# A new order table for a fused attention and feed-forward kernel on one core, and its last stores shared anew

## The chip, the core and the metric

The kernel runs on one core of one Trainium2 chip. A core has TensorE (matmuls, the page's PE, with its weight loads shown apart as PEld), VectorE (DVE), ScalarE (ACT), GpSimd (POOL) and SyncE (SP), and sixteen DMA engines. The metric is the device time of one execution in microseconds. Each run counts once; the median of the runs is compared.

## The reference, cut to what matters

```python
B, N, m, C = 4, 12480, 32, 128            # tokens: 4 x 12480 = 49920
def mab(q, kv):                           # attention
    s = (1 / sqrt(C)) * (q @ kv.T)
    a = exp(s - s.max(-1)); a /= a.sum(-1) + 1e-9
    return a @ kv
h = mab(inducing, x)                      # 32 x 128 for each of the 4 batches
y = mab(x, h)                             # 12480 x 128 for each batch
u = y @ w_in                              # 128 -> 2048
g = maximum(u, 0) + alpha * minimum(u, 0)
out = g @ w_out                           # 2048 -> 128, float32
```

## The kernel before, in words

Since `y = a @ h` with only 32 rows in `h`, the kernel folds `h @ w_in` into one 32 x 2048 matrix for each batch (`hW`, made in `h_weights`). A token's hidden values are then a matmul with 32 rows of contraction from its 32 unnormalized attention weights (`rep`), and a quarter of TensorE's array holds it. The leaky activation is split into a linear part, one matmul with `hA` straight from the attention weights (`linear`), and a ReLU part. The division by the sum of the weights comes last, on the output.

The tokens are cut into 100 groups, 25 to a batch: 24 of 512 tokens and one of 192. Each group has sixteen chunks of 128 hidden values (for the small group, two chunks share one eviction, so that it has eight). For every chunk a **fill** (`fill`, L733) makes one matmul into a bank of PSUM, and one engine evicts the bank with a ReLU into a bf16 tile `gt`: ScalarE at L750, VectorE at L752. Then the **second matmul** (`second`, L784) multiplies `gt` by `W1` and accumulates the 128 outputs in a bank that the group holds until it ends.

TensorE's array is split in four tiles of 32 rows, named w, x, y, z. A second matmul is cut into four, one on each tile, 32 hidden values each; they all add into the same bank. So tile w does all its sixteen of a group first, then x its sixteen, and so on, and between two tiles stands a **hand-over** (`hand_over`, L723): a no-operation in TensorE's queue that waits until the tile before has ended its last matmul of that group. The last three groups (`WHOLE`) aren't cut: their second matmuls take the full array.

When a group's last second matmul is out, `finish` (L809) transposes the bank on VectorE into `ot`, multiplies it by the reciprocal sums on GpSimd into `ob`, and stores `ob` with four DMAs of 32 partitions, on GpSimd's queue. For the last groups (`to_end` counts how many groups have yet to end) the scaling is shared with VectorE and the four stores go out on other queues. `ob` has three buffers, `ot` two.

The order of all this is written out by hand, or rather by characters, in the table `PLAN`. Every engine's instructions are pinned to the order in which the table names them:

- `a` to `h` with a digit: a fill on tile w (a, b), x (c, d), y (e, f) or z (g, h) into the bank of that number; the first letter of each pair evicts on ScalarE, the second on VectorE.
- `w`, `x`, `y`, `z`: the next second matmul of that tile. Each tile walks through the groups by itself.
- `v`: the next second matmul on the full array, in the last three groups. `l` and `m` with a digit: a group takes that bank, and its linear matmul on tile w opens it (`l` for the cut groups, `m` for the last three).
- `s` with digits: a **stop**, at which the table `PAUSES` has attention scores, denominators and the like done on the full array. [...]

A **letter** below is one entry of the table, its bank digit included. A group has 64 second matmuls, sixteen fills and one linear matmul, 81 letters.

Of the kernel before, what the change touches and what calls it, by code (L numbers as in the profile page):

```python
# [200 lines left out]
b02h12c223a312s4h212b012a323c12313f413s23e01h112l2wg42d33w231w3e03w32d1w31we431w3f31w3e01w32w3d1  # L201
2w3c42w32wd3g02w132w12h1wc4232xa02h3xa523x23b4x23a1x23xl0w23wxxwf3g5xw3e4s1h5xe3wxe4w3xwf13xw23x
wxe3wh5x2w32wc43wyd13wyc6wg3ys5b4yya1d6ywya5yyg3xb43xy3ya1xyxh6yc53yxh3ya4x3xy3xb1xza6zl5xe7zwxf
3zwc4wzwf1zxwe6zwh7xwzc3wzxwg4d1wzxwe6xzwf7zwzc3ywywzd4ywzc1yzl6yxwg7yxg3wxywh4xywxya1xywxyh2a7x
ywxyb3xya4xywd1ywxe2wxzf7s342zf1xwzxwe3zxwf7zwc2zwyc4zwyd1zwyzyc3zyxb7zyxg2yxb4zyxza1yxzyxb3ze7x
zyxl2yxwg4yxwyxwg1yxwh3yxwxg7wf4xzwxe0zwze1wzywd3zywzyc7wzyd4wzyc0wzwf1zwyza3yza7xyzb4xyza0xzyxl
1zyxwyxwg3yxwh7xywg4yxwh0xywg5xwzxe3wxzwf7xzwxze4wxf5zwc0zwzd3yws745d0wzywyzc3b7yzyzxa4yzxl5yzxb
0yzxa3yzxwzxywxg7ywxg4ywyxh0wyg3xwyxwyxh7wxe6wxzf4wxze0wxze3wzwd7zywc6zywzywd4zyc0zyxb3zyxzya7xz
yb6xzya4xzyl0xzywxg3ywxzywxg7ywxyh6wxywg4xe3wxzwxf2zwxzwe7xzwe4d6zwyzwyd3zwyzc2wyzd7wyza6yzl4xyz
wxyg3b2xyzxwyza6xyzb7xyzwxyg3wxyg2wxyh6ywxwxwxe7zs312xzb7e6xzwf3xzwe2xzwzwc1zywd6yzwc7yzwd2yzwza  # L210
3yzyb1xyzxa6zyxl7zyxwh2yxa3yxzwyxwg6yxwg1yxwyxwh3yxwg2xwe6xwzf5xwzxwze1xwzf3c2wzwzywd6yzwc5yzyzd
1yzb3xyzxa2yzxa6yxzl5yxzwyxza1yxzwyxg2wyxh3wyxg6wyxwyxh1wxe0wxze2wxzwxf3zwze6wzywzyc0wzyd1wzywc2
zyd3l6zyxwzya0xzyb1xzywxzya2zxyzxwys3012xh4ywxg3ywxywh0xywg2xe1wxwzf4xwzxwe3zxwzf2xwzc0wzd1wyzwy
c4zyza3yzxb2yzxl0yzxwyzc1b4yzxwyzxa3yzxwyg2xwyxwh1yxg4wyxwyxg3wyd7wxwe2zxwf1zxwzxwe4zxwf3zc7wzc2
ywzyd1zyxzya4xzb3yxza7yxzyxb2zyxzl1yxg4wyxwh3yxwg7yxzwyxzwyc2ywxg4yxwf3xwze7xwzxwf2s5437wyzd2wyz
c5wyzwyzd4we3zwyzb7yza2yzxya5zxyb4zxyl3zxywxzf7a2xzywxzywxg5ywxg4ywxyh2wxg7wxwxzf5wxze6wxze4wxzw
zd2wzywzc7ywzd6ywzyc5za4yzb2xyzxyl7zxywzxyb6g5xywzxywzxya4xywg2xywh6xywxywg5xwf4xwze0xwzf2xwze6x
wzwzd5ywzc4ywzc0ywzyl6zd2wzyxwzyxzya4xzyb5xzya0xzywxg2ywxzywxywh4xywg5xywxyg0wxs2154wxe0zwxf2zwx
e1zxwze4d5zwzywd0zywc2zyl1yzxwyzxa5zyxb4zyxwyzc2b0yzxwyzxa5yxwzyxwg4yxwg2yxwh0yxwyxwg5xwf4xzwe3x
zwxzwf2c0zwzd5ywyzwyzc4l3yzwxzya2xzyb0xzywxe5zwd4yzwxzya2xzywxzya0xywxh5ywxg4ywxywxg2ywxh0wxe7zw  # L220
xf4zwxzwe5c2zwyzwd0yzl7ywzxya4xzf5wzxywyzc2b0yzxwyzxa4yzxb5yzxwzyc2wzyxs0452ywxg0f6wxg4ywxg5ywxh
2ywxs0d6we4zxwzxwze5xwzf2c0wzd4zyl6yxzwxyza5xyzb2xyzwc0yzwxyzb4xyza5xyzwxyza2xyzwxywg0xyh4wxyg5x
wys21045wxywxh2e1wxf4zwc5zwyzwyc0zwyd1zwyc2zyzb5xyza4xyzl0xyzwxyza1xf2zwxzywxf4g5wxyzwxyza1xzywx
yg2wxyg5wxyh4wxwxf1zwxe3zwzwc2yzwyd5wzyc4wzyzl3d1yzwxyza2xyzwxf5zwxe4zwxyzb1xyza2xywzxyzwc5ywxyg
4wxyg1b2xywxywxe5b7xzwe4xzwd2zwxe1zwd5zwyc7zwyzc4yb2zxyl1zxywzxya5h7yxwzyxwg4d2ywzywxza5yxzyb7xz
xywg4ywxzywxg2yxwe5wxf7wzxf4xzws2657wxzf2wzc4wzyd6wzyc7l5zywwzxywwwzxe2b4zxywwzxywa7h6xywwxzywwx
zwe2wb4xyzwxwzya7xzyl6xywxg2ywxyh4wxywg7xywxwf0c2zwyxzxwxyxh4wc7yzxwyxzxwxe2d0zwyxzxwyxzwc7f4zxw
yxzxwyc2zb0yxzxxyza7xyzb4xyzxya2zxyzl0xywg7xywxyh4ywyxe2zwxyzwyxyyh3we7xzwyxyzywyxe4h2wxyzwyxyyz
wyc7f3zwyzwyc4zwyd2zwyzwc7yzyb3zxya4zxyzxa2yzxl7yzxzwyzzxa3zf4zxzwzyzxzwzyg2xywh1xwyzxg3wyxzzwxz
ze4wzxf2wzxwe1zxwzf3c5wzywzyc4wzyd2wzyc1zwyb3zyza5xyzxyb4zxya2zxyl1xzywxze3xwyh5xwyg4xwyxwyg2xwy  # L230
h3s6452xzwf3xzwe6xzwe4xzwf2xzwc5zwzwyd3wzywd6zywc4zya2zyl5zyxwh3yxwzyxwg4yxb6zyxwzyxa2yzxwyxwyg3
xwyxh4ya6xwe2xwxzf0wxzwxe3zwxzf6wzc4wzywd2zywc0zyzya3zxb6yzxyl4zxywzc2b0yzxywzxya3zxywg6xywxyh2w
xywg0xyg3wxywh7xwe6xzwxzwf2xzwe0xzwd3zwyzc7wyzwyza6d2yzl0xyzwxyg3wd7yzwxyzwxe6zb2xyzwxyza3xyzwxy
a7xywh6xyg2wxywxyg3wxf1wxwzxe7wzxf2zwc6zwyzwd3yzc1yzxa7yzxb2yzxl6yzxwyzc3b1yzxwyzxwyg7xb2yzxwyzx
we3zwxyg1wxywxywxh7ys23517xwzf2xwze3xwzf7c5wzwzyc1wzyd2wzya3zyzyxb7zyxa5zyxb1zyxl2zyxwze3xwzyd7w
yxg5wyxzwyxg1wyxg3wyxh7wyxwxg5wxzf1wxze4wxzwzd3wzyc7wzyd5wzyc1l4zyxwzyxa3zf7xwzyxwze1xzb5yxzwyxz
a3yxzwyxg7wyxwh1yxa5yxwg3yxwyxh0wyxwe7xwzf5wc1zywzywd3zywc0zya7zyxb5zyxl1zyxwzyc3b0zyxwzyxwg7f5x
wzyxwzyxa3zf0xwzyxwg7yxwzyxwg5yxwf3xwe0zxwzxwze7wd6zywzywc5yzd0l3zwxe7zwxzyb6xzywc5yzwxyzxb0yzxa
7zyxwyh6xa5yzxwyzxwyg0xwyxwg7yxwyh5xws60275h6we0xwzxwzd2e5zyc7wzywzyd0l6zyxwzyxa5zyd2wzyxwg7yxwz
f0xwzyxa5zyxwh2yxwze7xwzyxwh0yxa5yzxwyxza2yxg7wxwzxf0wze5wzywd2zywc4zya7zyxzb0yxzl5yxzwyxg2b4yxz  # L240
wyxzwyc7h0wyxzwyxza2yxh4wyxzwyc7zwyxzwe0xwf2zxwzxe4wzxwzxe7wzd0wzywzc1yl4zd2ywzxya7zxywh0xywzc1y
wzyxb2zyxa7zyxwzyxa0zyxwg1yxwyxwh2yxwg7yxwxf0we3xzwf1xzwze2xwzwzc7wyzd0yl3zwyxzya2xh1ywxzxya7zxy
b0zxywzc2wyzd1wyzxa7yzwxyzwxyg0wxyh2xwyg1wxye7wxwxzf0s6127f0zxwe6zxwzd1we7zwyzc2yzxyb0zxyzxya6zy
xb7zyxa1zyxl2zyd0wzyxwg6yxwh7yxwzyc1wzyxwg0yxwh6xywxwe7xzwxe1zwxzwf0c5zwyzwd7yzwc6yzwd1yza0yzxl5
yzxwyzxa7f6zxwyzxwyg0xb1yzxwyzxa7yzxwyg6xwyh0xwyxg1wyxwe7xwzxf4wzxe6wzwzyd1wzyc0wzyd7wzya4zya6xz
yxzb1yxzl0yxzwyd7zwe4xzwyxzwe6xzwyxg1wyxwh4yxwyg7xwyxh6wyxa3xe1wzxwzf4xwze7wzywzd3ywzc6yl1zyxwh4
yxwg7yxwzyxb3zyc6wzyxwzyxa4h7yxwzyxwzyd3a6zyxwzyxwg4yxwzxe7wzxwzxb6s34273e6wzd4f7wzxe2wzxs3yc6wz
yl4zd2ywzxya7zxzb3yxg6wyxywzxwyh2xyg7wxzwyxzb3yc6ywzxyzwxza2yxyg7wxwyxf6xg3wxwze2xwzf5zwzwyc7zwy
# [59 lines left out]
def kernel(  # L308
# [815 lines left out]
```

## Time and profile before

| | us |
|---|---|
| median of 3 runs | 541.08 |
| lowest and highest run | 541.07, 543.59 |
| span of the profiled execution | 540.4 |
| TensorE matmuls busy | 526.3 |
| VectorE, ScalarE, GpSimd busy | 504.2, 496.3, 394.7 |

The profiled execution's own time is its span, from its first to its last instruction; the page gives no other. The median of the runs lies 0.7 us above it. TensorE's granted clock is full throughout (0.996 on the mean). Matmuls overlap on the four tiles and their ends are modelled, so TensorE's busy share does not say how full it is; starts do. A row such as `bank<-gt,W 32*128 32x512` is a second matmul on one tile, `bank<-rep,hW` a fill, `bank<-rep,hA` a linear matmul, and `128*128` a matmul on the full array. In the timeline, neighbouring instructions of one name are merged into one row with their count.

### The profile page before, as it was taken

The numbers are of one execution on the slowest core, as the hardware profiler recorded it, in microseconds if no ns is written. First come the engines' busy times: TensorE is split into PE (matmuls) and PEld (weight loads), VectorE is DVE, ScalarE is ACT, GpSimd is POOL, SyncE is SP. The second block draws the span as 40 slices with busy tenths as digits, with TensorE's granted clock in tenths as the row PEclk, the third lists the DMA queues.
The fourth block names the chain that finished last, engine by engine and source line by source line (L and its number), as shares of the span: only waits on it lengthen the run. The fifth ranks groups of instructions, "written<-read, shape, count | busy, mean of one in ns | idle before, by whom it ended". The sixth has DMA issues, their size and how long they took to land.

```text
span 540.4 us, 21603 instructions
## 1 busy us (share of the span) xinstructions
PE 526.3 (97%) x8988; PEld 332.7 (62%) x8988; DVE 504.2 (93%) x865; ACT 496.3 (92%) x994; POOL 394.7 (73%) x574
## 2 busy tenths in 40 slices
PE   4999999999999999999999999999999999999996
PEld 4655566566567566666667666666666566666653
DVE  3699999999989999999998999999999999999994
ACT  2499999999989999999999999999999999999950
POOL 5553778687667987687687987776767876776764
PEclk9999999999999999999999999999999999999998
DMA  8999999987799898887799797864354344334324
GB/s 197 212 186 139 182 185 156 170 142 113 112 175 149 134 160 152 162 129 145 117 153 166 117 164 158 168 101 113 66 93 113 66 96 112 70 89 108 68 42 85
DMA packets 114738, 71.12 MB, mean 132 GB/s; under 512 B 86784, under 2 KB 102784, under 8 KB 114640
## 3 DMA queue, kind: packets, MB, share of 16 engines
q0 software_dynamic: 19456, 38.62, 38.9%
q1 hardware_dynamic: 91984, 30.22, 32.9%
q8 instruction: 70, 1.15, 0.9%
q10 hardware_dynamic: 3200, 0.90, 0.7%
q14 instruction: 28, 0.23, 0.2%
HBM read 41.00 MB, written 28.95 MB: 129 GB/s over the span
## 4 chain that ended last, share of the span: by engine, by line
PE 90%; DMA 4%; DVE 2%; ACT 1%; POOL 1%; issue 1%; SPq 0%; POOLq 0%; DVEq 0%
PE bank L383 90%; DMA xn<-in_x_dram 2%; DMA rep<-e2d 1%; ACT gt L750 1%; DVE gt L752 1%; DMA e2d<-e 1%; POOL xn L412 0%; DVE ot L818 0%; PE bank L458 0%; ACT e L656 0%; DVE xT L461 0%; POOL ob L826 0%; DVE fr L608 0%; SPq L671 0%; POOL out_dram L851 0%
## 5 line engine op out<-in xcount | busy, mean ns | idle before, releaser
L383 PE MATMUL bank<-gt,W 32*128 32x512 bf16 (+1 forms) x6256 | 480.3, 371 | 0.1
L750 ACT ACTIVATE gt<-bank 128x512 bf16<-128x512 f32 (+1 forms) x906 | 464.5, 612 | 6.9 <-PE bank L383 4.6
L752 DVE TENSOR_SCALAR gt<-bank 128x512 bf16<-128x512 f32 (+1 forms) x662 | 417.7, 677 | 9.9 <-PE bank L383 6.1
L383 PE MATMUL bank<-rep,hW 32*128 32x512 bf16 (+1 forms) x1600 | 418.4, 368 | 1.5 <-DMA rep<-e2d 1.3
L383 PEld LDWEIGHTS <-W 32*128 32x128 bf16 x6256 | 264.4, 92 | 146.5 <-issue 46.6
L851 POOL DMA_DIRECT2D out_dram<-ob x386 | 247.3, 669 | 37.7 <-POOL ob L826 30.4
L826 POOL TENSOR_TENSOR ob<-ot,rdT 128x512 f32<-128x512 f32 (+2 forms) x99 | 106.3, 1074 | 93.8 <-DVE ot L818 79.5
L383 PEld LDWEIGHTS <-hW 32*128 32x128 bf16 x1600 | 136.9, 92 | 20.8 <-issue 5.1
L818 DVE STREAM_TRANSPOSE ot<-bank 128x512 f32<-128x512 f32 (+1 forms) x100 | 69.9, 699 | 6.7 <-PE bank L383 5.6
L383 PE MATMUL bank<-rep,hA 32*128 32x512 bf16 (+1 forms) x100 | 36.1, 367 | 0.0
L427 POOL DMA_DIRECT2D xn<-in_x_dram x32 | 20.7, 663 | 0.1
L481 ACT ACTIVATE e1t<-bank 128x256 bf16<-128x256 f32 (+2 forms) x14 | 5.0, 356 | 10.8 <-PE bank L383 10.8
L461 DVE COPY xT<-bank 128x1024 bf16<-128x1024 bf16 (+1 forms) x13 | 8.5, 650 | 4.9 <-PE bank L458 4.4
L383 PE MATMUL bank<-xT 32*128 32x512 bf16 x81 | 12.5, 376 | 0.0
L553 ACT ACTIVATE e<-bank 128x512 bf16<-128x512 f32 x18 | 11.0, 610 | 0.2 <-PE bank L383 0.2
L656 ACT ACTIVATE e<-bank 128x512 bf16<-128x512 f32 x18 | 11.1, 614 | 0.1
L383 PEld LDWEIGHTS <-xT 128*128 128x128 bf16 (+1 forms) x177 | 8.0, 97 | 4.1 <-issue 1.5
L383 PEld LDWEIGHTS <-hT 128*32 128x32 bf16 (+1 forms) x122 | 3.6, 93 | 11.0 <-issue 10.9
L383 PE MATMUL bank<-xT,hT 128*32 128x512 bf16 (+1 forms) x98 | 10.3, 388 | 0.0
L383 PEld LDWEIGHTS <-hA 32*128 32x128 bf16 x100 | 9.2, 92 | 1.8 <-issue 0.6
L458 PE MATMUL bank<-ident,xn 128*128 128x128 bf16 x96 | 9.0, 249 | 1.0 <-DVE xn L963 0.9
L412 POOL DMA_DIRECT2D xn<-in_x_dram x11 | 6.2, 583 | 3.3 <-DMA xn<-in_x_dram 2.5
(87 smaller groups left out, 131.7 us busy)
## 6 DMA issues: line engine op xcount, KB each, us to landing
out_dram<-ob POOLq DMA_DIRECT2D x373, 64.0 KB, 3.2
rep<-e2d SPq DMA_DIRECT2D x92, 128.0 KB, 3.2
xn<-in_x_dram POOLq DMA_DIRECT2D x37, 256.0 KB, 5.5
e2d<-e SPq DMA_DIRECT2D x24, 128.0 KB, 3.6
xn<-in_x_dram POOLq DMA_DIRECT2D x4, 512.0 KB, 8.2
rdT<-rt SPq DMA_DIRECT2D x96, 8.0 KB, 2.6
early<-in_moe_w_out_dram POOLq DMA_DIRECT2D x4, 256.0 KB, 10.6
xT<-xn SPq DMA_TRANSPOSE x36, 5.2
```

Source lines behind the costliest of these rows:

```text
L383: return pin(nc.tensor.matmul(o, lhsT, rhs, start=start, stop=stop, **kw))
L412: pin(nc.gpsimd.dma_start(out=xn[:, q0:q1, :], in_=src[:, q0:q1, :]))
L427: pin(nc.gpsimd.dma_start(out=st.xn[u][:, part, :], in_=src[:, part, :]))
L458: pin(nc.tensor.transpose(tp[:, k * P : (k + 1) * P], xn[:, q, j * C : (j + 1) * C], ident[:]))
L461: pin(nc.vector.tensor_copy(out=st.xT[:, u, qs[0] : qs[-1] + 1, :].rearrange("c q t -> c (q t)"), in_=tp[:, : len(qs) * GRP],))
L553: pin(nc.scalar.activation(out=e1[:], in_=ps[:], func=EXP, scale=scale, accum_out=st.es[:, u : u + 1]))
L656: pin(nc.scalar.activation(out=e2[:].rearrange("p (t j i) -> p t j i", j=n, i=32), in_=turned(ps[:pp, :w], n), func=EXP, scale=scale_of(st ...
L750: pin(nc.scalar.activation(out=gt[:, :w], in_=ps[:, :w], func=RELU))
L752: pin(nc.vector.tensor_relu(gt[:, :w], ps[:, :w]))
L818: pin(nc.vector.transpose(out=ot[:, :t], in_=acc[:, :t]))
L826: pin(engine.tensor_tensor(out=ob[:, k0 * w : k1 * w].rearrange("p (k m c) -> p k m c", k=k1 - k0, c=32), in0=ot[:, k0 * w : k1 * w].rearr ...
L851: pin(queue.dma_start(out=dst[a], in_=ob[32 * a : 32 * a + 32, :t].rearrange("p (b k) -> p b k", k=32),))
```

## The change

The table `PLAN` has the same length in characters and the same second matmuls, stops and linear matmuls, and 1568 fills as before; from its 274th character on the order is another one, with other banks and another choice of the evicting engine (914 on ScalarE and 654 on VectorE, where it was 906 and 662). In the last 700 letters, fills and evictions of both engines stand nearly to the end, and the matmuls on the full array are spread between them in thirteen pieces. Before, ScalarE had its last eviction ahead of all of them, and they came in three pieces of sixteen.

In `finish`, `store` writes a group with one DMA over all 128 partitions on GpSimd's queue; for the third last group to end it goes to ScalarE's queue. The last but one has the first half scaled on GpSimd, and its other half is held back: VectorE does it after the last group, and two DMAs then store it, on ScalarE's and GpSimd's queues. The last group is scaled on VectorE and stored by one DMA on SyncE's queue.

The end of the two tables, and `finish`:

```diff
@@ PLAN @@
...
-zwyc4zyxzb7yxza1yxzyb2xyzl0xyzwxyza4xyh7xwzyc1wzywxzyxwg2yxwh4ywxyg7wyxs1d5e2zwxzwxzwe7zwxf4zwe
-1zwyc2zwyd5zwyd7zya4zxya1zxyzxyb2zxyg5xyzd4yg7xyzxyh1xya2zxyxyg5xyh4xe7xzxf2zxe1zxzc5e6zyzb7yzyb
-4zc1yzyzyh5yh2yb6zyd7zyzyzyh1ym4zyb5zvvvvvvvvvvvvvvvvyd2m6h7yh1d5vvvvvvvvvvvvvvvvzzd3m4zzzzzf2zz
-zzb7f1b5zzzzzvvvvvvvvvvvvvvvv
...
+c7yd0zwyyyza2zxzyyb6zxxyxa4yl0zwd7zwwyxxyyxg2zzzb6c4xwyxyxxwg7wh2wwyzwwyg6xywe4xxzzzs7zxxwzwe2zf6wwc
+3yywyzzzd4d7yyc2yg6zxxyyza3xyzxyxxxyzb4yb2yxxg7xzg6ym3zvvva4xxh7yzyxze2vve6zzzxxb7xvva4yzzyyg1vva2h7
+yyyzzvvb6yzzc4zyyyc7g1vvvd2zyzyzyzvvm4yyg6yzzvvc7zf1zzf2e6ze3vvvvvc5zh7zzb1vvvvb6e2h3zzzc7vvvvvm5zzz
+vvve1zzzvvvvvvvvvvvvv
@@ finish @@
...
-        if to_end == 0:
-            scaled(nc.vector, 0, nb)
-        elif to_end == 1:
-            scaled(nc.gpsimd, 0, nb // 2)
-            scaled(nc.vector, nb // 2, nb)
-        else:
-            scaled(nc.gpsimd, 0, nb)
...
-        queues = {
-            3: (nc.sync,) * 4, 2: (nc.scalar,) * 4,
-            1: (nc.sync, nc.scalar, nc.gpsimd, nc.sync),
-            0: (nc.scalar, nc.gpsimd, nc.scalar, nc.sync),
-        }.get(to_end, (nc.gpsimd,) * 4)
-        for a, queue in enumerate(queues):
-            pin(queue.dma_start(
-                out=dst[a],
-                in_=ob[32 * a : 32 * a + 32, :t].rearrange("p (b k) -> p b k", k=32),
-            ))
...
+        def store(*queues):
+            n = NQ // len(queues)
+            for k, queue in enumerate(queues):
+                pin(queue.dma_start(
+                    out=dst[n * k : n * k + n],
+                    in_=ob[32 * n * k : 32 * n * (k + 1), :t].rearrange("p (b k) -> p b k", k=32),
+                ))
+
+        def rest():
+            scaled(nc.vector, nb // 2, nb)
+            store(nc.scalar, nc.gpsimd)
+
+        if to_end == 0:
+            scaled(nc.vector, 0, nb)
+            store(nc.sync)
+            for fn in held:
+                fn()
+        elif to_end == 1:
+            scaled(nc.gpsimd, 0, nb // 2)
+            held.append(rest)
+        else:
+            scaled(nc.gpsimd, 0, nb)
+            store(nc.scalar if to_end == 2 else nc.gpsimd)
```

More of the change, by code (lines that the diff above doesn't have):

```diff
@@ L807 @@
     ended = [0]
+    held = []
     def finish(st, g, acc):
@@ L818, in finish @@
         pin(nc.vector.transpose(out=ot[:, :t], in_=acc[:, :t]))
-        ob = ob_pool.tile([P, GRP], f32, name="ob", tag="ob")
         to_end = B * NG - 1 - ended[0]
         ended[0] += 1
-        def scaled(engine, k0, k1):
-            w = t // nb
-            part = rbc[:, k0:k1]
-            pin(engine.tensor_tensor(
-                out=ob[:, k0 * w : k1 * w].rearrange("p (k m c) -> p k m c", k=k1 - k0, c=32),
-                in0=ot[:, k0 * w : k1 * w].rearrange("p (k m c) -> p k m c", k=k1 - k0, c=32),
-                in1=part, op=MULT,
-            ))
-        if to_end == 0:
-            scaled(nc.vector, 0, nb)
-        elif to_end == 1:
-            scaled(nc.gpsimd, 0, nb // 2)
-            scaled(nc.vector, nb // 2, nb)
-        else:
-            scaled(nc.gpsimd, 0, nb)
         t0 = st.b * N + s * SUP
```

202 lines of the change are left out of this document (102 added, 100 removed).

## The prediction

> **What bounds the kernel now.** I read the page, then the busy time by stretches, then TensorE's timeline in short windows, and last the chain and the rows of the end.
>
> ```profile
> PE 526.3 (97%) x8988; PEld 332.7 (62%) x8988; DVE 504.2 (93%) x865; ACT 496.3 (92%) x994; POOL 394.7 (73%) x574
> PE 90%; DMA 4%; DVE 2%; ACT 1%; POOL 1%; issue 1%; SPq 0%; POOLq 0%; DVEq 0%
> ```
> ```profile
> 450.00:500.00 50.00, 50.00 (x859) 31.44 (x853) 49.74 (x83) 49.96 (x98) 36.77 (x51) 1.00 0.41 97
> 500.00:520.00 20.00, 19.99 (x322) 12.05 (x317) 19.82 (x34) 19.88 (x41) 14.87 (x22) 1.00 0.31 60
> 520.00:530.00 10.00, 10.00 (x70) 4.52 (x65) 7.88 (x15) 0.26 (x1) 6.64 (x9) 1.00 0.28 54
> ```
>
> Three engines look full to 520 us. From there ScalarE does nothing and TensorE goes on alone. The chain lies on TensorE for 90%. Busy time overlaps within an engine, so I look at starts. First the pace of one row tile (letters w, x, y, z of the order table):
>
> ```profile
> 178.94 0.38 PE L383 MATMUL bank<-gt,W 32*128 32x512 bf16 x3
> 178.95 0.37 PE L383 MATMUL bank<-rep,hW 32*128 32x512 bf16 x1
> 179.15 0.38 PE L383 MATMUL bank<-gt,W 32*128 32x512 bf16 x3
> 179.16 0.37 PE L383 MATMUL bank<-rep,hW 32*128 32x512 bf16 x1
> 179.37 0.38 PE L383 MATMUL bank<-gt,W 32*128 32x512 bf16 x3
> ...
> 529.31 0.81 PE L383 MATMUL bank<-gt,W 32*128 32x512 bf16 x3
> 529.75 0.33 PE L383 MATMUL bank<-rep,hW 32*128 32x192 bf16 x2
> 529.96 1.02 PE L383 MATMUL bank<-gt,W 32*128 32x512 bf16 x4
> ```
>
> Four matmuls, one on each tile, start together and the next four about 0.216 us later; a run on one tile has the same step ((1.02 - 0.37) / 3). So one letter costs 0.216 / 4 = 0.054 us while all four tiles are fed.
>
> Second, the hand-over of a bank (`hand_over`, L723): the next tile's first matmul of a group waits until the tile before has ended its last one.
>
> ```profile
> 341.03 0.46 PE L383 MATMUL bank<-gt,W 32*128 32x512 bf16 x3
> 341.24 0.37 PE L383 MATMUL bank<-rep,hW 32*128 32x512 bf16 x1
> 341.30 0.41 PE L383 MATMUL bank<-gt,W 32*128 32x512 bf16 x2
> 341.36 0.37 PE L383 MATMUL bank<-rep,hW 32*128 32x512 bf16 x1
> 341.46 0.46 PE L383 MATMUL bank<-gt,W 32*128 32x512 bf16 x3
> ...
> PEld L383 <- PE bank L383: 12.7, 57, 0.4
> ```
>
> The table has `xwze4wzd7y` here. At 341.03 tile x starts its last matmul of a group; seven letters later tile y starts its first, at 341.46: 0.43 us, where seven letters are worth 0.38. Between 341.36 and 341.46 nothing starts on any tile: the wait stands in the one queue of TensorE, and all behind it waits too. The last row is the idle time of the weight loads that ended with a matmul's end, at most 0.4 us each.
>
> Third, a stop of the table (here scores and denominators of the next block):
>
> ```profile
> 487.43 0.37 PE L383 MATMUL bank<-rep,hW 32*128 32x512 bf16 x1
> 487.73 0.40 PE L383 MATMUL bank<-xT,hT 128*32 128x512 bf16 x4
> 488.06 0.25 PE L383 MATMUL bank<-pick,e 128*128 128x4 bf16 x4
> 488.25 0.39 PE L383 MATMUL bank<-gt,W 32*128 32x512 bf16 x3
> ```
>
> It takes 0.82 us from the last fill to the next row matmul, 0.6 more than a step. Now the account of 450 to 500 us: 859 matmuls, less 2.5 stops of eight, are 839 letters x 0.054 = 45.3; stops 1.5; the old table has 276 hand-overs with no stop inside, worth 11.8 us in all (below), 0.043 each, and three in 81 letters, so 31 here: 1.3. Together 48.1 of 50 us. TensorE's order by itself explains 96% of a stretch in which both evicting engines also look full. The order is therefore what I cost.
>
> **The change part by part.** *The hand-overs.* In both tables I counted the letters from a tile's last matmul of a group to the next tile's first, without those that have a stop between. Old, 5 to 8 letters: 5, 51, 89, 69 times, never fewer than 5. New, 2 to 8: 6, 10, 14, 23, 35, 44, 48 times. A distance d leaves 0.435 - 0.054 d us (0.435 is my reading of the 0.43 above): 0.327, 0.273, 0.219, 0.165, 0.111, 0.057, 0.003 for 2 to 8. Old: 0.8 + 5.7 + 5.1 + 0.2 = 11.8 us. New: 2.0 + 2.7 + 3.1 + 3.8 + 3.9 + 2.5 + 0.1 = 18.1 us. Difference +6.3. The long distances, 95 against 62 with nine letters or more, give nothing back, since the wait is already zero there. What could cover this is work that the tiles hold queued; the account above needed the full 11.8 us, so I take +6.3, with bounds of -11.8 (all hand-overs covered) and +7.3 (at the 0.058 us per matmul that 50 / 859 gives).
>
> *Runs on one tile.* Two neighbouring letters of one tile: 89 in the old table, 1190 in the new (836 runs of two, 141 of three, 24 of four). Whether a run stops the other tiles is seen where `m4` enters:
>
> ```profile
> 520.32 0.39 PE L383 MATMUL bank<-rep,hA 32*128 32x512 bf16 x1
> 520.43 0.59 PE L383 MATMUL bank<-gt,W 32*128 32x512 bf16 x3
> 520.70 0.37 PE L383 MATMUL bank<-rep,hW 32*128 32x512 bf16 x1
> 520.86 0.37 PE L383 MATMUL bank<-gt,W 32*128 32x512 bf16 x1
> ```
>
> In the table `yzyh1y` stand ahead of `m4`, and all five start after it. At 529.75 a fill starts while three z ahead of it have yet to start. So a tile holds up to three waiting matmuls and lets the others pass: runs of two to four are nearly free. Bounds 0 and 24 x 0.216 = 5.2 us (each run of four stops the queue for one step); I take +0.5, near the end that the rows show.
>
> [...]
>
> *The last 700 letters.* Behind the last stop the old table has 15 fills for ScalarE and 26 for VectorE, the new one 24 and 16; ahead of it 891 and 636 against 890 and 638. So where engines look full, nothing moves. Of what comes behind, the matmuls of tile z and the full-array matmuls (`v`) can't overlap: 58 + 48 in the old table, 56 + 48 in the new.
>
> ```profile
> 512.06 0.21 PE L383 MATMUL bank<-pick,e2r 32*96 32x1 bf16 x2
> 512.32 0.44 PE L383 MATMUL bank<-rep,hW 32*128 32x512 bf16 x2
> ...
> 528.13 1.34 PE L383 MATMUL bank<-gt,W 128*128 128x512 bf16 x5
> 529.09 0.25 PE L383 MATMUL bank<-rep,hW 32*128 32x192 bf16 x1
> ...
> 534.78 0.97 PE L383 MATMUL bank<-gt,W 128*128 128x192 bf16 x5
> ...
> 535.86 0.38 DVE L818 STREAM_TRANSPOSE ot<-bank 128x192 f32<-128x192 f32 x1 [1.46 <-PE bank L383]
> 536.28 0.36 DVE L826 TENSOR_TENSOR ob<-ot,rdT 128x192 f32<-128x192 f32 x1
> 536.94 0.54 POOL L851 DMA_DIRECT2D out_dram<-ob  x1 [0.44 <-DVE ob L826]
> ```
>
> Old: 58 x 0.216 = 12.5, 32 `v` x 0.216 = 6.9, 16 narrow ones x 0.16 ((0.97 - 0.33) / 4) = 2.6. Between full-array and row matmuls there is a step that is longer: the group at 528.13 is four `v` and one z, so the fourth `v` starts at 528.78, and the row matmuls at 529.09: 0.31, 0.095 above the step. The old table has 5 such changes, 0.5 us: 22.5 in all, against 23.5 measured (512.32 to 535.86), so 1.0 us of other waits. The new one has 25, as `v` come in 13 pieces: 12.1 + 6.9 + 2.6 + 2.4 = 24.0. Bounds +0.5 (the other waits vanish) and +1.5; I take +1.0. ScalarE evicting to the end gains nothing here: VectorE's last transpose waited 1.46 us for TensorE, not the reverse.
>
> [...]
>
> *Stores.* One DMA in place of four.
>
> ```profile
> L851 POOL DMA_DIRECT2D out_dram<-ob x386 | 247.3, 669 | 37.7 <-POOL ob L826 30.4
> L427 POOL DMA_DIRECT2D xn<-in_x_dram x32 | 20.7, 663 | 0.1
> L826 POOL TENSOR_TENSOR ob<-ot,rdT 128x512 f32<-128x512 f32 (+2 forms) x99 | 106.3, 1074 | 93.8 <-DVE ot L818 79.5
> out_dram<-ob POOLq DMA_DIRECT2D x373, 64.0 KB, 3.2
> xn<-in_x_dram POOLq DMA_DIRECT2D x37, 256.0 KB, 5.5
> ```
>
> A 256 KB load costs GpSimd 0.66 us, like a 64 KB store: one store lies between 0.67 and 4 x 0.67 = 2.7 us, no more than now, and GpSimd already waits 79.5 us for transposes. Its landing, 3.2 to 5.5 us, must fit into the three `ob` buffers, one group of about 4.8 us (81 / 839 x 50) each: it fits. Steady worth: 0; without that cover, up to 2.1 us late for one group.
>
> The store of the third last group to end moves in its queue: it now stands on ScalarE ahead of the last eviction (`e1`). It waits for that group's transpose (0.72) and GpSimd's scaling (1.07), issues in about 0.65, and behind it come the eviction and the last two `v`. That is some 3.5 us after the group ends with the eviction (0.5) and semaphores; ahead of those two `v` TensorE has six z, three and eleven narrow `v` and four changes, 1.3 + 2.2 + 0.4, with a linear and a fill some 4.3 us. Covered by 0.8, so 0; if one store of GpSimd in front costs 2.7 us, up to +1.9.
>
> The final group's own path is as now, and then VectorE does half of the group before (0.42 now, at 533.97) and two 128 KB stores go out on ScalarE and GpSimd, 1.4 us after the last matmul; the last store of now goes out 1.5 us after it. Bounds -0.1 and +0.9 (landing by the larger size); 0.
>
> *Other waits.* Banks are filled again sooner: 188 refills within fewer than 17 letters, 66 before. The account leaves 1.9 us in 50 for all such waits, 17 us over 460. They could halve, as a later TensorE finds tiles evicted, or grow by half: -8 to +8; with reasons on both sides I take 0.
>
> **Sum:** 6.3 + 0.5 + 1.0 = +7.8 us, on the profiled span 540.4: 548.2. The median of the runs is 541.08, 0.7 above that span, so 548.9.
>
> **The rivals.** *A: the queued runs bridge the hand-overs.* A tile with three waiting matmuls has 0.65 us of work, more than 0.435. If the new runs leave tiles so filled at hand-overs, the wait costs nothing there. For it: the rows at 520.32. Against it: the old order, at 341.36, had nothing queued. With 80% covered the stalls are 18.1 x 0.2 = 3.6, against 11.8: -8.2, with runs and end +1.5: 541.1 - 6.7 = 534.4. It decides from a cover of 43%, where stalls are 10.3 and the sum is nil.
>
> *B: no change.* Cover of a third to a half, or other waits shrinking by what the stalls add: 541, within 2.7.
>
> *C: strict order of matmuls over the tiles.* Each of 1101 added neighbours then costs 0.216 - 0.054 = 0.162 us: +178, about 719 us. Only if what passes at 520.32 and 529.75 were an exception. [...]
>
> *D: the tiles share a small common queue.* If at most five waiting matmuls may be passed (the 520.32 row shows five, none shows more), runs in two tiles block each other. Priced as a half step for each of the 165 runs of three or four: 18 us, 567.
>
> **How the numbers follow.** Forecast 0.60 (548.9), A 0.19, B 0.14, C 0.02, D 0.05. About 0.5% (2.7 us) is what a measurement can tell from no change: faster 0.19, same 0.14, slower 0.67. Upper end: hand-overs 6.3, runs 5.2, end 1.5, half of the growing waits 4: +17, 558; C and D lie above, 0.07. Lower end 535, with half of A, about 0.1, below. If slower, 543.8 to 558.
>
> **What would show it.** Matmuls from 450 to 500 us fall from 859 to about 847. The wait of weight loads for a matmul's end grows from 12.7 us and 57 times, past 18. Row matmuls start before others of another tile more often, with runs on one tile 0.216 apart. From the first fill behind the last stop to the last transpose: 24 to 25 us in place of 23.5. ScalarE's last eviction moves from 520 to within 6 us of the end. GpSimd's time in stores falls. I am wrong if those 50 us hold more than 865 matmuls: then tiles ran through the hand-overs.

## The result: 1509 us, and the profile after

| | before | after |
|---|---|---|
| median of the runs, us | 541.08 (540.21 to 543.59, 4 runs) | 1509.22 (1502.87 to 1519.36, 4 runs) |
| span of the profiled execution, us | 540.4 | 1508.9 |
| TensorE matmuls busy, us | 526.3 | 809.3 |
| GpSimd busy, us | 394.7 | 453.7 |
| mean granted clock | 0.996 | 0.712 |

The ratio is 2.787 (95% interval 2.775 to 2.800). Forecast were 548.9 us, range 535 to 558, and no rival came near. Line numbers have moved: the store stands on L838 now, the scaling on L829, the transpose on L815, ScalarE's eviction on L746, VectorE's on L748, the matmuls on L379.

Of the page, the line of the engines, the queue of GpSimd's DMAs, the shares of the chain, three groups (count, busy time, mean of one, then idle time ahead of them and who ended it) and the landing of the stores:

```profile
PE 809.3 (54%) x8985; PEld 427.4 (28%) x8988; DVE 522.1 (35%) x857; ACT 536.9 (36%) x1002; POOL 453.7 (30%) x286
q0 software_dynamic: 33280, 41.27, 42.6%
issue 70%; POOL 21%; DMA 4%; PE 2%; SPq 1%; POOLq 0%; DVE 0%; ACT 0%; DVEq 0%
L838 POOL DMA_DIRECT2D out_dram<-ob x98 | 303.9, 3102 | 1013.0 <-issue 936.0
L815 DVE STREAM_TRANSPOSE ot<-bank 128x512 f32<-128x512 f32 (+1 forms) x100 | 70.3, 703 | 730.8 <-POOL ob L829 713.5
L829 POOL TENSOR_TENSOR ob<-ot,rdT 128x512 f32<-128x512 f32 (+2 forms) x99 | 146.1, 1480 | 17.8 <-DVE ot L815 17.8
out_dram<-ob POOLq DMA_DIRECT2D x94, 256.0 KB, 14.8
```

No engine is full. The chain that was 90% TensorE is 70% "issue" and 21% GpSimd. One store takes 3.1 us of GpSimd where one of the four took 0.67, and lands after 14.8 us, not 3.2. Above all GpSimd idles 936 us ahead of its stores, and nothing that the profile shows ends that wait. GpSimd's own timeline (start, duration, idle before) shows what does:

```profile
601.77 3.14 POOL L838 DMA_DIRECT2D out_dram<-ob  x1 [10.30 <-issue]
604.50 1.00 POOL L423 DMA_DIRECT2D xn<-in_x_dram  x1
605.08 1.52 POOL L829 TENSOR_TENSOR ob<-ot,rdT 128x512 f32<-128x512 f32 x1
615.47 3.15 POOL L838 DMA_DIRECT2D out_dram<-ob  x1 [8.87 <-issue]
618.23 1.49 POOL L829 TENSOR_TENSOR ob<-ot,rdT 128x512 f32<-128x512 f32 x1
630.13 3.13 POOL L838 DMA_DIRECT2D out_dram<-ob  x1 [10.41 <-issue]
```

The next scaling is done within 5 us, and then the next store stands until about 14 us after the last one began, which is when that one has landed: in the trace, 89 of the 97 stores behind the first begin 0.28 to 0.40 us after the landing of the store ahead of them. A load of 256 KB in between takes 1.0 us and waits for nothing. So a group takes some 15 us, and 98 stores make nearly all of the span. The list of waits (total us, times, longest) shows how it gets to TensorE:

```profile
POOL out_dram L838 <- issue: 936.0, 87, 13.9
DVE ot L815 <- POOL ob L829: 713.5, 90, 14.2
PE bank L379 <- DVE ot L815: 614.0, 87, 11.1
```

The store holds the scaling behind it, the scaling holds the `ot` buffer that the next transpose needs, VectorE's evictions stand behind that transpose, and TensorE's fills wait for their banks.

### The profile page after: what moved, and what is told of

Same layout as the page of the kernel before. It is cut to its first block, busy times and chain, and to the rows that moved or that the text cites. A ratio compares the mean times of both kernels' runs of the same rounds, so it can differ in the third digit from the quotient of the medians.

```text
span 1508.9 us, 21332 instructions
## 1 busy us (share of the span) xinstructions
PE 809.3 (54%) x8985; PEld 427.4 (28%) x8988; DVE 522.1 (35%) x857; ACT 536.9 (36%) x1002; POOL 453.7 (30%) x286
## 4 chain that ended last, share of the span: by engine, by line
issue 70%; POOL 21%; DMA 4%; PE 2%; SPq 1%; POOLq 0%; DVE 0%; ACT 0%; DVEq 0%
POOL out_dram L838 11%; POOL ob L829 8%; PE bank L379 2%; POOL xn L423 2%; DMA out_dram<-ob 1%; DMA rt<-rd 1%; DMA xn<-in_x_dram 1%; DMA rep<-e2d 1%; SPq L667 1%; DMA rdT<-rt 0%; POOLq L1122 0%; POOLq L829 0%; POOL xnr L411 0%; POOL xn L408 0%; ACT gt L746 0%
## 5 line engine op out<-in xcount | busy, mean ns | idle before, releaser
L379 PE MATMUL bank<-rep,hW 32*128 32x512 bf16 (+1 forms) x1600 | 568.3, 483 | 536.5 <-DVE ot L815 525.0
L746 ACT ACTIVATE gt<-bank 128x512 bf16<-128x512 f32 (+1 forms) x914 | 501.9, 596 | 844.1 <-PE bank L379 786.7
L379 PE MATMUL bank<-gt,W 32*128 32x512 bf16 (+2 forms) x6253 | 751.2, 476 | 36.1 <-ACT gt L746 32.9
L838 POOL DMA_DIRECT2D out_dram<-ob x98 | 303.9, 3102 | 1013.0 <-issue 936.0
L379 PEld LDWEIGHTS <-W 32*128 32x128 bf16 x6256 | 364.3, 110 | 785.3 <-issue 647.2
L748 DVE TENSOR_SCALAR gt<-bank 128x512 bf16<-128x512 f32 x654 | 430.8, 681 | 206.3 <-PE bank L379 198.2
L815 DVE STREAM_TRANSPOSE ot<-bank 128x512 f32<-128x512 f32 (+1 forms) x100 | 70.3, 703 | 730.8 <-POOL ob L829 713.5
L379 PEld LDWEIGHTS <-hW 32*128 32x128 bf16 x1600 | 151.5, 106 | 122.7 <-issue 106.1
L829 POOL TENSOR_TENSOR ob<-ot,rdT 128x512 f32<-128x512 f32 (+2 forms) x99 | 146.1, 1480 | 17.8 <-DVE ot L815 17.8
L379 PE MATMUL bank<-rep,hA 32*128 32x512 bf16 (+1 forms) x100 | 51.4, 517 | 0.3 <-ACT gt L746 0.3
L379 PE MATMUL bank<-pick,e 128*128 128x4 bf16 x96 | 6.1, 168 | 31.9 <-DVE ot L815 31.9
L379 PE MATMUL bank<-xT,IT 128*32 128x512 bf16 x72 | 9.6, 502 | 18.3 <-DVE ot L815 18.1
L379 PE MATMUL bank<-xT,hT 128*32 128x512 bf16 (+1 forms) x98 | 12.1, 460 | 13.0 <-DVE ot L815 12.5
L379 PEld LDWEIGHTS <-e 128*128 128x128 bf16 x96 | 4.6, 101 | 39.5 <-issue 39.2
L379 PEld LDWEIGHTS <-hT 128*32 128x32 bf16 (+1 forms) x122 | 4.1, 96 | 37.2 <-issue 37.1
L379 PE MATMUL bank<-xT 32*128 32x512 bf16 x81 | 12.5, 376 | 0.0
L379 PEld LDWEIGHTS <-hA 32*128 32x128 bf16 x100 | 11.6, 116 | 2.9 <-issue 1.9
L379 PE MATMUL bank<-xnr,e1Tr 96*32 96x128 bf16 x6 | 1.0, 265 | 16.6 <-DVE ot L815 16.6
## 6 DMA issues: line engine op xcount, KB each, us to landing
out_dram<-ob POOLq DMA_DIRECT2D x94, 256.0 KB, 14.8
```

The costliest lines, as they stand in the source:

```text
L379: return pin(nc.tensor.matmul(o, lhsT, rhs, start=start, stop=stop, **kw))
L746: pin(nc.scalar.activation(out=gt[:, :w], in_=ps[:, :w], func=RELU))
L748: pin(nc.vector.tensor_relu(gt[:, :w], ps[:, :w]))
L815: pin(nc.vector.transpose(out=ot[:, :t], in_=acc[:, :t]))
L829: pin(engine.tensor_tensor(out=ob[:, k0 * w : k1 * w].rearrange("p (k m c) -> p k m c", k=k1 - k0, c=32), in0=ot[:, k0 * w : k1 * w].rearr ...
L838: pin(queue.dma_start(out=dst[n * k : n * k + n], in_=ob[32 * n * k : 32 * n * (k + 1), :t].rearrange("p (b k) -> p b k", k=32),))
```

## The experiments

Each is compared with runs of the kernel before on the same chip.

### The two parts of the change apart

`e1_four_stores`: the changed kernel, steady stores in four DMAs again; table and ending as changed.

```diff
-            store(nc.scalar if to_end == 2 else nc.gpsimd)
+            store(*((nc.scalar,) if to_end == 2 else (nc.gpsimd,) * 4))
```

> The new table and the new ending as they are, but each group of the steady part stored by four DMAs of 64 KB on GpSimd's queue, as in the kernel before. Theory 1 (the single store of 256 KB holds GpSimd's queue for some 14.5 us a group, and everything else waits for it): the excess goes, and what is left is the order table alone: 549 us by the working of the prediction (535 to 558). Theory 2 (the new order itself runs into long waits, and the stores are only where they show): still above 1400 us. Between the two, some 700 to 1000, both would have a part.

Measured: 628.37 us, ratio 1.159 (1.156 to 1.162).

`e2_old_table_one_store`: the kernel before, with one DMA per group on GpSimd in the steady part.

```diff
-        }.get(to_end, (nc.gpsimd,) * 4)
+        }.get(to_end, (nc.gpsimd,))
+        n = NQ // len(queues)
...
```

> The kernel before with its own table, and one DMA of 256 KB in place of four for every group on GpSimd's queue; the last four groups are stored as before. Theory 1: about 96 groups x 14.6 us + the head of some 50 us = 1450 us (1400 to 1550). Theory 2: 541 us, at most a few us off.

Measured: 1476.72 us, ratio 2.721 (2.709 to 2.732). Its page has the same row:

```profile
L852 POOL DMA_DIRECT2D out_dram<-ob x98 | 299.0, 3051 | 988.0 <-issue 915.5
```

What follows: the single store alone makes the kernel 2.7 times as long. Behind it something else hides: the table and the ending, without the single store, cost 86 us, eleven times what I had forecast. There are two causes to find.

### What is dear in the single store

`e3_two_stores`: two DMAs of 128 KB, two blocks of 32 columns each (`(nc.gpsimd,) * 2`); `e4_one_store_on_sync`: the one DMA on SyncE's queue (`nc.sync`). Both with the new table.

> The changed kernel with two DMAs of 128 KB (64 partitions each) for a group. If the cost is in the form of the DMA (a destination that goes over several blocks of 32 columns): each half takes half of the 14.6 us, about 1500 us as before. If it is in the size alone, beyond a number of rows of 128 bytes that two halves stay below: about 549 us. In between (each half pays less than half): 700 to 1200.

> The changed kernel with the single store of 256 KB on SyncE's queue. If only GpSimd's way of issuing such a DMA is slow: near 549 us, plus what the loads behind the store on SyncE's queue lose by its wait for the scaling, up to 40 us: 549 to 600. If the transfer itself is slow on any queue (rows of 128 bytes in four blocks): about 14 us a group again, above 1200 us.

Measured: 2787.81 us for two stores, ratio 5.136 (5.119 to 5.153), and 933.95 us on SyncE, ratio 1.721 (1.713 to 1.728). A line of the first, then two of the second:

```profile
L838 POOL DMA_DIRECT2D out_dram<-ob x195 | 599.0, 3078 | 1996.6 <-issue 1968.8
```
```profile
q1 hardware_dynamic: 284584, 54.84, 39.5%
L379 PE MATMUL bank<-rep,hW 32*128 32x512 bf16 (+1 forms) x1600 | 479.4, 408 | 140.3 <-DMA rep<-e2d 137.9 <-DVE gt L748 0.7 <-ACT gt L746 0.5
```

Neither run came out as I had expected it. Half the bytes cost GpSimd the same 3.1 us and the same wait, where I had expected half of it, so the price is one for each DMA and not for its size: twice the DMAs, nearly twice the time. On SyncE the time lies between my two values. The queue carries 284584 packets in place of before's 91984, the fills wait 138 us for `rep`, which comes on the same queue, and GpSimd's scalings wait 247 us in all for stores to land.

`m1_order_and_stores_alone` has nothing of the kernel: orders of matmuls (below), and GpSimd stores of one 128x512 tile in four forms, each three times in a row (L90, in four DMAs, twice).

```diff
+    # L94: as the change stores, four blocks of 32 columns
+    for q in range(3):
+        pin(nc.gpsimd.dma_start(out=four(1, q), in_=ob[:].rearrange("p (b k) -> p b k", k=32)))
...
+    # L99: the same 2048 pieces of 128 bytes, in one block
+    for q in range(3):
+        dst = out[SUP * (2 + q) : SUP * (3 + q), 0:32].rearrange("(p b) k -> p b k", b=16)
+        pin(nc.gpsimd.dma_start(out=dst, in_=src))
...
+        # L104: 2 KB of a partition in one piece; L109: so too, in four blocks of partitions
```

> Not the computation: row matmuls of 32x128 weights and 32x512 columns with no waits, in eleven written orders, each closed by a full-array matmul; beside them GpSimd stores of one 128x512 tile in four forms. Orders, per letter, for runs of 1, 2, 3, 4 and 6 letters on one tile (w, x, y, z in turn). My prediction's theory, three matmuls may wait on each tile and all others pass: 0.054, 0.054, 0.054, 0.054, 0.081 us; 384 letters out of the new table 25.0 us, out of the old one 24.4. Rival, only one may wait on a tile: 0.054, 0.054 to 0.056, 0.076, 0.112, 0.148; 28.4 to 29.5 and 26.1 us. Rival, strict order over the tiles: 0.054, 0.110, 0.146, 0.164, 0.182; 35.6 and 27.2 us. Stores: if the form is dear (one transfer whose destination lies in four blocks of 32 columns), the new form holds GpSimd until the landing of the one before, some 14 us each, and the same 2048 rows of 128 bytes in one column block land in 3 to 6 us one after another; if the number of rows of 128 bytes is what costs, both take some 14 us and only the transfers with 2 KB in one piece are quick.

GpSimd's timeline:

```profile
24.49 3.12 POOL L94 DMA_DIRECT2D out_dram<-ob  x1
37.87 3.12 POOL L94 DMA_DIRECT2D out_dram<-ob  x1 [10.25 <-issue]
52.85 3.09 POOL L94 DMA_DIRECT2D out_dram<-ob  x1 [11.86 <-issue]
130.35 3.46 POOL L99 DMA_DIRECT2D out_dram<-ob  x3
208.21 1.62 POOL L104 DMA_DIRECT2D out_dram<-ob  x3
284.24 2.12 POOL L109 DMA_DIRECT2D out_dram<-ob  x3
```

The form is dear, not the count of pieces. With no computation to wait for, stores of the new form stand 13 to 15 us apart, while the same 2048 pieces of 128 bytes in one block go out three in 3.5 us. Four blocks with one piece of 2 KB for each partition go out three in 2.1 us. `m2_signal_order` (below) adds two: four blocks with pieces of 512 bytes, three in 4.7 us (L98), and two blocks with pieces of 128 bytes, 15 us apart (L106). Of the forms tried, only those hold the next store that have both several blocks of partitions and sixteen pieces of 128 bytes in each partition. (The cheap forms with four blocks do land late, 6.8 to 11.1 us after their start with three under way, but they hold nobody.) Nor does the program make one store wait for the next: in both traces each waits at most for the semaphore of the DMA eight before it, which had long landed.

```profile
22.96 4.69 POOL L98 DMA_DIRECT2D out_dram<-ob  x3
104.50 3.12 POOL L106 DMA_DIRECT2D out_dram<-ob  x1
119.51 3.11 POOL L106 DMA_DIRECT2D out_dram<-ob  x1 [11.88 <-issue]
```

In the packets of these DMAs each form with several blocks has 192 or 224 small packets beside its data, of 8 bytes for each piece of a partition: 8 bytes at one piece, 32 at four, 128 at sixteen, where one lasts about 0.31 us against 0.01. The forms with one block have none. How many packets are under way at once says more. Of the data packets it is four for 62 to 74% of the time with four blocks (never more than five), two for 87 to 90% with two blocks, and up to sixteen or more with one block. The small packets of the dear forms reach twelve and fourteen at once, and 192 is 16 x 12, 224 is 16 x 14. As an estimate from these counts, four or two of the sixteen DMA engines move the data, and each of the others has sixteen small packets. No row names the engine, and what the small packets carry no view tells.

### What is dear in the table

`t1_old_table_with_runs` and `t2_new_table_fewer_runs` move the letters w to z only between two other entries of the table. A piece of the old table, before and after:

```diff
-f0zxwe6zxwzd1we7zwyzc2yzxyb0zxyzxya6zyxb7zyxa1zyxl2zyd0wzyxw
+f0zxwe6zxwzd1we7zwyzc2yzxyb0zzyyxxa6zyxb7zyxa1zyxl2zyd0wwyxz
```

> The kernel before, with the letters w to z moved only between two other entries of the table so that neighbours on one tile are 1428 in place of 86; fills, banks, stops and all hand-over distances stay. Three waiting per tile: 542 (+1). One waiting per tile or in all: +13 to +33, 555 to 575. Strict order: each of 1342 added neighbours costs up to 0.162, toward 700. If early refills of banks are what the new table suffers from, nothing changes here: 542.

> The new table with four stores per group (628), its letters w to z moved in the same way so that neighbours on one tile fall from 1162 to 418; hand-overs, fills, banks as in the new table. If runs carry the 86 us one for one: 69% of it goes, 568. One waiting per tile: 608 to 612. Three waiting per tile, or early refills as the cause: 627, no change.

Measured: 543.26 us (ratio 1.002, 0.999 to 1.004) and 628.35 us (1.156, 1.150 to 1.161). Runs on one tile cost nothing, in either table. `m1` says why; the rows are stretches from the first matmul of an order to the full-array one behind it (length, busy time of TensorE, its loads, VectorE and GpSimd, then the granted clock), with runs of 1, 2, 3, 4 and 6, and at the end 384 letters of the old and of the new table:

```profile
14.87:20.16 5.29, 5.29 (x97) 2.39 (x97) 0.00 (x0) 5.12 (x4) 1.00 0.01 3
20.32:25.62 5.30, 5.30 (x97) 2.63 (x96) 0.00 (x0) 5.18 (x4) 1.00 0.01 3
25.79:31.10 5.31, 5.31 (x97) 2.80 (x97) 0.00 (x0) 1.83 (x1) 1.00 0.39 21
31.26:36.60 5.34, 5.34 (x97) 3.08 (x97) 0.00 (x0) 0.00 (x0) 1.00 0.66 36
36.76:44.91 8.15, 8.15 (x97) 4.11 (x96) 0.00 (x0) 3.12 (x1) 1.00 0.32 13
...
76.23:102.84 26.61, 26.61 (x385) 12.53 (x384) 0.00 (x0) 25.75 (x16) 0.92 0.01 2
103.00:128.24 25.24, 25.24 (x386) 13.21 (x385) 0.00 (x0) 24.49 (x14) 1.00 0.01 2
```

Up to runs of four, 96 letters take 5.3 us, 0.055 each; at six 8.15, 0.085 each. Three matmuls do wait on a tile while others pass. Without waits the new order takes 25.2 us. The old one took 26.6 at a clock of 0.92, which at full clock would be some 24.5 as an estimate, so the new order by itself is some 3% slower, not 16%. So the loss is in waits between engines, and the trace of `e1` has them. The waits of the evictions for a fill, of the kernel before and of `e1`:

```profile
DVE gt L752 <- PE bank L383: 6.1, 18, 1.4
ACT gt L750 <- PE bank L383: 4.6, 9, 1.5
```
```profile
DVE gt L748 <- PE bank L379: 60.8, 164, 1.5
ACT gt L746 <- PE bank L379: 57.5, 157, 1.7
450.00:500.00 50.00, 49.21 (x719) 25.99 (x713) 41.71 (x67) 42.75 (x81) 32.43 (x47) 1.00 0.34 75
```

Both evicting engines idle 58 to 61 us for TensorE, and TensorE, at the full clock, does 719 matmuls in these 50 us where it did 859, so it is held up as well. From the start of a fill to the start of its eviction, where the evicting engine had been idle, the starts in `e1`'s trace give a median of 0.78 us (349 times); before, it was 0.42 (52 times). The fill has started, but the engine that evicts it begins late.

A new theory: **ends are told in program order**. A matmul that passes others starts early, but its end reaches the other engines only when all that stand ahead of it in the program have ended. A second micro-kernel measures it: `m2_signal_order` writes short orders and evicts what tile x wrote.

```diff
+ORDERS = ['x', 'wx', 'wwx', 'wwwx', 'wwwwx', 'xwww', 'wwwzzyx']
...
+            g = const.tile([P, GRP], bf16, name="g", tag=f"g{n % 2}{len(order)}{order}")
+            if n < 3:
+                pin(nc.scalar.activation(out=g[:], in_=banks[1][:], func=COPY))
```

> Not the computation: short written orders of row matmuls (x; wx; wwx; wwwx; wwwwx; xwww; wwwzzyx), after each an eviction of the bank that tile x wrote, by ScalarE in three rounds and by VectorE in three; the next order waits for it. The measure is the time from the start of the x matmul to the start of its eviction. Theory, the end of a matmul is told to the other engines only when all that stand before it in the program have ended: 0.41 us for x, wx and xwww, 0.62 for wwx, 0.84 for wwwx, 1.06 for wwwwx, 0.84 for wwwzzyx, though x itself starts beside the first w. Rival, each matmul tells its own end: 0.41 in all seven. GpSimd stores beside them: if four dimensions of the destination are dear, the transfer in four blocks with pieces of 512 bytes also holds the next one for some 14 us; if pieces of 128 bytes in several blocks are, it takes 1 us or less and lands in 3 to 6; two blocks of 32 columns (128 KB) should cost like four, one block (64 KB) 0.7.

ScalarE and TensorE in a timeline, the orders `wwwx`, `wwwwx` and `xwww`; the first matmul of each waits for the eviction before and has its own row:

```profile
18.39 0.58 PE L64 MATMUL bank<-g,W 32*128 32x512 bf16 x1 [0.69 <-ACT g L78]
...
18.40 1.42 PE L64 MATMUL bank<-mov,W 32*128 32x512 bf16 x3
...
19.86 0.60 ACT L78 ACTIVATE g<-bank 128x512 bf16<-128x512 f32 x1 [1.53 <-PE bank L64]
20.51 0.58 PE L64 MATMUL bank<-g,W 32*128 32x512 bf16 x1 [0.69 <-ACT g L78]
...
22.41 0.60 ACT L78 ACTIVATE g<-bank 128x512 bf16<-128x512 f32 x1 [1.96 <-PE bank L64]
...
23.06 0.58 PE L64 MATMUL bank<-g,W 32*128 32x512 bf16 x1 [0.69 <-ACT g L78]
...
23.68 0.60 ACT L78 ACTIVATE g<-bank 128x512 bf16<-128x512 f32 x1 [0.67 <-PE bank L64]
```

`xwww` and `wwwx` are the same four matmuls, and in both x starts within 0.01 us of the first w. Its eviction begins 0.62 us after that in the one, 1.47 in the other, which is 0.67 after the third w starts. (The granted clock was 0.50 here, so a step on one tile is 0.43 us and not 0.216; the first round began at a clock of 1.00 and has 0.41 us for `x`, 0.43 for `wx`, 0.63 for `wwx`.) `wwwwx` has 1.90, and `wwwzzyx` 1.54, near `wwwx` as the theory has it. VectorE's three rounds agree within 0.07 us. In these orders only the matmul of x raises the semaphore that the eviction waits for, so the wait isn't one for a count that the others bring up. The theory's order and steps came out, the rival's equal times did not.

Now its price in the kernel. `t3_old_table_unbalanced_at_fills` exchanges second matmuls of two tiles, also across a fill, so that at fills more matmuls of other tiles stand queued ahead. Fills, banks, stops and hand-overs stand where they stood:

```diff
-f0zxwe6zxwzd1we7zwyzc2yzxyb0zxyzxya6zyxb7zyxa1zyxl2zyd0wzyxw
+f0xzze6wxzzd1we7wwyyc2zzxyb0yyxyyxa6xzzb7zzya1xzxl2zyd0wyxzy
```

`t4_new_table_rebalanced` goes the other way in the new table. There fills move too, by a few places; the distances of the hand-overs stay:

```diff
-zwxzxzwf1wzc7f2wyyzzc3xza6xyb1yyxzl7wxyzc2f3zxywzxwya6b1wyyz
+xwzzxf1wc7wf2zzwyc3zzyxa6yxzxb1yzyl7wzzxyc2f3yzwyzxwxya6zb1y
```

> The kernel before, with pairs of letters w to z exchanged, now also across a fill; every fill, bank number, stop and hand-over stands at its old place in the table, so refills are as early as before. At the fills more matmuls of other tiles stand queued ahead. Theory of ends told in program order: a count over the table gives +34 us, and as that count gave 56 of the 86 us of the new table, up to +52: 577 to 595. Rival, each matmul tells its own end: +3, 545. Early refills of banks as the cause of the new table's loss: no change, 542.

> The new table with four stores per group (628), letters w to z and fills exchanged with neighbours (at most 8 places) so that fewer matmuls of other tiles stand queued ahead of fills; hand-overs at their old distances, neighbours on one tile 1319 against 1162. Theory of ends told in program order: -22 us by the count, up to -33: 595 to 606. Rival, each matmul tells its own end: +4, 632. Early refills (74 within 17 letters against 85): 625 to 628.

Measured: 584.90 us for t3, ratio 1.077 (1.073 to 1.081); 615.74 us for t4, 1.133 (1.129 to 1.137), against `e1`'s 1.159. The waits of t3:

```profile
DVE gt L748 <- PE bank L379: 32.0, 119, 0.8
ACT gt L746 <- PE bank L379: 25.4, 90, 0.7
```

t3 costs 41.5 us, within the theory's 34 to 52, where the rivals gave 3 and 0. Its neighbours on one tile, some 1160 by a count over the table, can't be the cause: t1 has some 1430 and costs nothing. It is moving matmuls across a fill that counts. t4 falls as only this theory has it, but by 12.6 us and not by 22 to 33: the count overrates what a rebalancing of that table brings.

### The hand-overs, and the ending

`t5_old_table_short_hand_overs` moves the first letter of a tile's group up to five places closer to the hand-over (`c2yzxy` becomes `c2xyzy`). `e5_new_table_all_stores_in_blocks` is `e1` with the last stores one DMA for each block, too:

```diff
-            store(nc.scalar, nc.gpsimd)
+            store(nc.scalar, nc.scalar, nc.gpsimd, nc.gpsimd)
...
-            store(nc.sync)
+            store(*(nc.sync,) * 4)
```

> The kernel before, with the first letter of a tile's group moved 0 to 5 places closer to the last letter of the tile before it; fills, banks and stops stay, 151 neighbours on one tile against 86. By the price of the prediction (0.435 - 0.054 d per hand-over) stalls rise from 11.8 to 34.8 us: +23, 565. A count over the table in which evictions and stops cover some of them gives +18: 559 to 561. If queued matmuls bridge the hand-overs: 541 to 544.

> The new table with four stores per group in the steady part (628), and now the last group's store and the two half stores of the group before it also as one DMA per block of 32 columns, on the same queues. In that kernel 20.8 us lie between the end of the last transpose and the end, against 4.2 before. If the half store on GpSimd (two blocks in one DMA, 128 KB) is what lasts: 610 to 613. If the end is bound by the landing of any last store: 626 to 630.

Measured: 560.03 us for t5, ratio 1.032 (1.028 to 1.037); 616.41 for e5, ratio 1.136 (1.132 to 1.139), 12.0 less than `e1` and 3.4 above the first of my two values. t5's row beside the one of before in the prediction (12.7 us, 57 times), then the last rows of `e1` and of `e5`:

```profile
PEld L379 <- PE bank L379: 59.1, 168, 0.6
```
```profile
602.85 1.16 ACTq L838 DMA_DIRECT2D out_dram<-ob  x1
604.13 0.49 ACT L746 ACTIVATE gt<-bank 128x384 bf16<-128x384 f32 x1 [4.58 <-DMA out_dram<-ob]
604.68 0.33 PE L379 MATMUL bank<-gt,W 128*128 128x192 bf16 x2 [1.60 <-ACT gt L746]
605.14 0.38 DVE L815 STREAM_TRANSPOSE ot<-bank 128x192 f32<-128x192 f32 x1 [2.25 <-PE bank L379]
607.10 3.15 POOL L838 DMA_DIRECT2D out_dram<-ob  x1 [3.51 <-DVE ob L829]
```
```profile
604.82 0.38 DVE L815 STREAM_TRANSPOSE ot<-bank 128x192 f32<-128x192 f32 x1 [2.28 <-PE bank L379]
606.81 1.29 POOL L838 DMA_DIRECT2D out_dram<-ob  x2 [3.56 <-DVE ob L829]
```

t5 costs 17.9 us for stalls that the prediction's formula puts at 23: three quarters of the formula is paid. In `e1` the half store on GpSimd has the dear form as well. From the end of the last transpose (605.52) to the end of the span (626.3) it takes 20.8 us, in `e5` 9.0, and 4.2 before. GpSimd's last packets end at 622.0, those of the other half (on q10, by its bytes ScalarE's queue) at 624.4; `e5` splits both, and the last group's store too, so the 12.0 us are not told apart. The ScalarE store in front of its last eviction holds TensorE for 1.60 us.

## Why the prediction was wrong, point by point

**Stores: the step that failed.** I put one store of 256 KB between 0.67 and 2.7 us of GpSimd, "no more than now", by the row of the 256 KB load, and its landing at 3.2 to 5.5 us, so its worth at 0. The store takes 3.1 us and the next one waits for its landing, some 15 us a group; `e2` has 934 us for it alone. The row that I scaled from has another form: the destination of the store lies in four blocks of 32 columns with sixteen pieces of 128 bytes in each partition, and no DMA of the kernel before has both. In a nearest row the form has to be looked at, not the bytes: the upper end had to be open here. And I priced the issue alone, not a wait of one store for the landing of the one before. Of the signs, GpSimd's time in stores should have fallen; it rose from 247.3 to 303.9 us, with 936 us of waits ahead of it. The matmuls from 450 to 500 us, 847 by my forecast, were 291, and 719 in `e1`.

Why the form is dear is shown in part. With four blocks four data packets are under way at once, with two blocks two, and half the bytes take as long (2787.81 us in `e3` for twice the stores): 64 data packets over four are sixteen each, and so are 32 over two. What the small packets beside the data do, and why the next store waits for the landing, stays open: `m1` and `m2` show for which forms it does.

**The order of TensorE.** "A tile holds up to three waiting matmuls and lets the others pass: runs are nearly free" was right, with +0.5 us for 1101 added neighbours: `t1` measured +0.4 us for 1342 (within its interval, so it may be nothing) and `m1` the same pace up to runs of four. Rival C, strict order, and D are out. What I missed is that it holds for starts alone.

Against strict order in the starts speaks `m1`, with 5.3 us for 96 letters in runs of one to four alike; for the order of the ends speaks `m2`, with 0.62 us from x to its eviction in `xwww` and 1.47 in `wwwx`. The two rows that I had read, at 520.32 and 529.75, speak of starts, and the forecast priced no order of the ends.

**Other waits: the second step that failed.** I took 0, with -8 to +8. By what is left over they are most of the table's loss. (The refills that I counted there don't bear on the sum, but the count is off: from one entry that names a bank to the next, stops left out, 129 come within fewer than 17 letters, where the old table has 65.) An order that lets one tile run ahead delays what the others' fills tell, and with it evictions, banks, and the next fills. As an estimate: a count over the table, with the paces of the traces (a step of 0.2155 us, three waiting on a tile, evictions 0.478 and 0.600 us apart, 0.41 us from a fill to its eviction), gives 56 us for the new table with ends told in order, 4 without. For t3 it gave 34 where 41.5 were measured, so it is low by a fifth; 56 by the same factor is 68. Of `e1`'s 86 us, 12.0 are the ending's stores, 1.6 the eviction behind ScalarE's store, 4.8 the rest of the ending (9.0 against 4.2), and 67 remain. The sizes agree as far as such an estimate goes; by `t4`, where 12.6 us came of 22, it would be too high. How these 67 divide between the order of the ends, the hand-overs, and the new choice of banks and evicting engines was not measured in the new table itself, so this cause is shown by `m2` and `t3`, and its share in the 67 us is not.

**Hand-overs.** +6.3 by a price of which t5 paid 78%, so some +4.9. t5's table has few runs, so against rival A, that queued runs bridge the hand-overs, speaks `e1`: its weight loads wait 30.0 us for a matmul's end, where before it was 12.7. The sign that I had named for it, past 18 us, came, with no bearing on the size.

**The ending.** "The final group's own path is as now", with +0.9 at most for the larger DMAs, failed as *Stores* did: 12.0 us, and 4.8 more behind the last transpose that `e5` leaves. For ScalarE's store ahead of the last eviction I took 0 and named +1.9 for the case that GpSimd is late; TensorE waited 1.60. From the first fill behind the last stop (579.30 in `e1`) to the last transpose it is 25.8 us, 2.3 more than before; less those 1.6 that leaves 0.7, inside the +0.5 to +1.5 of *The last 700 letters*.

**What bounds the kernel.** 48.1 of 50 us explained by TensorE's order was a sum that fitted, and I read it as leaving no room for the evictions. But four in ten fills of the kernel before start 0.05 us after their bank's last eviction ends, and VectorE and ScalarE were 99% busy in that stretch: three engines ran in step, and in `e1` all three lost (from 450 to 500 us VectorE was 83% busy, ScalarE 86%, and TensorE did 719 matmuls for 859).

## What to carry to other kernels

Price a DMA by its form, here the blocks of partitions in its destination and the pieces in a partition (three stores in 1.6 to 4.7 us, or one every 13 to 15), and where no row of the trace has that form, leave the upper end open and try it alone. Where small matmuls pass each other on the tiles of the array, look at when their ends are told, not only at their starts: a fill whose eviction is waited for belongs ahead of, or level with, what the other tiles have queued (`t3`, with more queued ahead of its fills, cost 41.5 us). A sum that explains nearly all of a stretch, here 48.1 of 50 us, does not show that the other engines have slack.

## What the runs showed of the hardware that I had not expected

- A GpSimd store into two or four blocks of 32 columns with sixteen pieces of 128 bytes for each partition takes 3.1 us of GpSimd and holds the next store 10 to 12 us more, at 128 KB as at 256 KB (here two and four data packets under way at once, and 224 and 192 small packets); with pieces of 512 bytes or 2 KB, or with one block, three such stores go out in 1.6 to 4.7 us.
- On SyncE's queue the same store makes, by the count, a packet of each piece: 284584 packets against 91984, 192600 more, where 94 stores of 2048 pieces are 192512.
- Matmuls on different tiles start out of order, three waiting on each (`m1`: 0.055 us a letter up to runs of four, 0.085 at six), but in the seven orders of `m2` their ends are told in order: 0.62 us from x to its eviction in `xwww`, 1.47 in `wwwx`, at a granted clock of 0.50.
